# Moving the down projection of the last 512 rows into the blocked products at the end, with another layout for the query weight scan

## The chip, the cores and the metric

The kernel runs on one core of a Trainium2 chip. Its time is device microseconds from one execution; what is compared is the median of several. Five engines work beside each other, each through its own queue in order: TensorE (PE, matrix products; PEld is its weight load), VectorE (DVE), ScalarE (ACT), GpSimd (POOL) and SyncE (SP, which only issues DMAs here). They meet through semaphores.

## The reference, cut to what matters

```
x  = A_x                                  # 2048 x 640, bf16
xn = layernorm(x)
# A: attention, 32 heads of 192, over the last 512 keys of the cache
q  = xn @ wq                              # 640 -> 32 * 192
s  = softmax(q k^T / sqrt(192)) v  @ wo   # 6144 -> 640
# B: gated block, F = 1536
h  = sigmoid(xn @ w_gate) * (xn @ w_up)   # 2048 x 1536
g  = silu(h @ w_down)                     # 1536 -> 640, the down projection
out = x + s * g
```

All inputs and the output are bf16.

## The kernel before

The kernel has three parts, and PE goes through them one after the other.

**Gates (lines 275 to 581).** The 2048 rows are taken in four lots `s` of 512 rows. For each lot the 12 blocks `f` of 128 gate columns are computed: ten products of 128 x 512 into a pair of PSUM banks (line 487), then a sigmoid on ACT (L492) and a multiplication on DVE (L493), which writes the tile `hT_sb`. A ring of four bank pairs (`bank2`) lets PE run ahead of ACT and DVE. The tile `hT_sb` has two buffers. For the first three lots the h rows are stored to the tensors `h_d` in memory (L550, and L530 for the third lot), and their down projection is done at the end of the kernel. For the fourth lot the down projection follows at once (L556 to L581): 96 products with `hT_sb` as weights and `wd_sb` as moving operand, a sigmoid into `sg`, a multiplication into `gB_sb`, and a DMA to `gB_d`.

Beside the gates other work is hung on steps `(s, f)` by small tables written out by hand, so the order of each engine's queue is the order of the code:

- `ln_at`: layer norm of the next lot; `ln_rest` (L438) turns the rows by a DMA transpose into `xnT`, which is in the tile `x_odd` for odd lots.
- `scan_load`, `scan_fold`, `scan_act`: the largest magnitude of the query weights is needed for a scale. Sixteen blocks of `wq` are loaded (L201) and reduced, on DVE (`scan_fold`) or as a sum of magnitudes on ACT (`scan_abs`, L300). `set_scale` turns the result across partitions with a small DMA transpose, `set_scale2` makes the scale `w_up`.
- `load_raw`, `scale_w`, `sum_w`: each of five chunks of a group's query weights is loaded (L230), scaled to fp16 (L244 and two copies, L249) and combined into sums (four operations on DVE, L262 to L266, and a copy on ACT). Queries are computed by a Winograd form of Strassen's blocked product, which needs these sums and those of x.
- `swap` and `sum_x`: the sums of x for two lots together, six operations of 64 x 2560 each on DVE.
- `load_k`, `scale_k`, `turn_k`, `load_v`: keys and values of the first group.

In the fourth lot, chunk 4 of the weights, two scalings for the next group (`scale_raw(1, ...)`) and three sums of x stand between the parts of the down projection (L569 to L577).

**Attention (lines 614 to 969).** Sixteen runs, one for each of 8 groups and 2 halves of the rows. Each computes scores (L700), exponentials (L704), the product with the values (L714), and the queries of the next run (L606, with evacuations at L625, L627 and L644). The queries of the first run are computed ahead of it, by `query_slots(0, True, ...)` at L772: there the copies are on ACT, and PE has the banks 2 and 3, 4 and 5, 0, 1 and 6. The tiles of this part (`qT`, `qp`, `E`, `o_st`, `oT`) lie in memory that the tiles of the gates had.

**Dense end (from line 971).** A list `steps` of blocked products, seven quarter products in place of eight: `O` steps for the output projection (7 x 12 products of 128 x 320 each), `D` steps for the down projection of two row tiles (7 x 6 products). `load_quads` loads the operands two steps ahead, `scale_quad` and `sum_quad` scale and combine them, `result` evacuates; for `D` steps it makes a gate and stores it to `gB_d`. Other work is hung on positions of the steps with `at`: `load_op`, `scale_op`, `sum_op` for the second half of the output weights, `pair_load` and `prep` for the gate and x rows of each tile.

```
steps = [(k[0], int(k[1:])) for k in "O0 O1 D0 D1 O2 D2 D3 O3 D4 D5 O4 O5 O6 O7".split()]
...
        if kind == "D":
            return (m, TQ + m) if m < TQ else (2 * m, 2 * m + 1)
```

Of the kernel before, what the change touches and what calls it, by code (L numbers as in the profile page):

```python
# [8 lines left out]
AF = mybir.ActivationFunctionType  # L9
ALU = mybir.AluOpType  # L10
# [7 lines left out]
def kernel(  # L18
# [75 lines left out]
    NH, NM3 = NF // 2, 3  # L94
    h_d = [dram.tile([P, NF, P], BF16, name=f"h_d{t}") for t in range(NM3 * TQ)]
# [51 lines left out]
    wq_n = A_wq.rearrange("(c p) n -> p c n", p=P)  # L147
# [42 lines left out]
    NPC, NSB = 16, 7  # L190
    NSC = NG * GC // NPC
    assert NSC <= GC // 2

    def scan_load(i, eng):
        n = i % NSB
        if n < 3:
            t = (XA, XB, XC)[n][1]
            scan_t[i] = (t if n == 2 else t.bitcast(BF16))[:, :, 0:NSC]
        else:
            scan_t[i] = w_even[n - 3].bitcast(BF16)[:, :, 0:NSC]  # L200
        eng.dma_start(scan_t[i], wq_n[:, :, i * NSC:(i + 1) * NSC])  # L201
# [73 lines left out]
    with ExitStack() as bctx:  # L275
# [4 lines left out]
        gpool = bctx.enter_context(tc.tile_pool(name="gpool", bufs=4))  # L280
# [10 lines left out]
        x_odd = xt_pool.tile([P, NCD, 512], BF16, name="x_odd")  # L291
        xnT = [x_even[0], x_odd, x_even[1], x_odd]

        wmax = bone.tile([P, NCD, NSC], BF16, name="wmax")
# [46 lines left out]
        wd_sb = wB.tile([P, NF, D], BF16, name="wd_sb")  # L341
# [101 lines left out]
        def swap(pi):  # L443
            x_sw = xt_pool.tile([P, 2, NCD, 512], BF16, name="x_sw")
            nc.sync.dma_start(XC[pi][LO], x_odd[HI])
            nc.sync.dma_start(XC[pi][HI], x_odd[HI])
            nc.sync.dma_start(x_sw[HI, 0], x_even[pi][LO])
            nc.sync.dma_start(x_sw[HI, 1], x_odd[LO])
            return x_sw

        def sum_x(pi, k, x_sw):
            ev, od, tt = x_even[pi], x_odd, nc.vector.tensor_tensor
            xa, xb = XA[pi], XB[pi]
            if k == 0:
                tt(xa[LO], od[LO], XC[pi][LO], ALU.add)
            elif k == 1:
                tt(xa[HI], od[HI], x_sw[HI, 1], ALU.add)
            elif k == 2:
                tt(xa[LO], xa[LO], ev[LO], ALU.subtract)
            elif k == 3:  # L460
                tt(xb[HI], xa[HI], x_sw[HI, 0], ALU.subtract)
            elif k == 4:
                tt(xb[LO], ev[LO], od[LO], ALU.subtract)
            elif k == 5:
                tt(xb[HI], ev[HI], xb[HI], ALU.subtract)

        sums = {(1, 4): (0, 4), (1, 10): (0, 0), (1, 11): (0, 1), (2, 7): (0, 2), (2, 9): (0, 3), (2, 10): (0, 5),
                (3, 2): (1, 0), (3, 4): (1, 1), (3, 7): (1, 2)}
        folds = {(1, 7): 9, (1, 8): 10, (1, 9): 11}
        scan_act = {(0, 7): 0, (0, 8): 1, (0, 9): 2, (0, 10): 3, (1, 1): 4, (1, 2): 5, (1, 3): 6, (1, 6): 7, (1, 7): 8,  # L470
                    (2, 0): 12, (2, 1): 13, (2, 5): 14, (2, 7): 15}
        scan_loads = {(0, 8): (4, 5, 6), (0, 9): (7,), (0, 10): (8,), (0, 11): (9,), (1, 1): (10, 11), (1, 7): (12, 13), (1, 9): (14, 15)}
        abs_at = [(0, 3), (0, 4), (2, 9), (2, 10)]
        ln_at = {0: (2, (1, 1, 2), 5), 1: (0, (1, 1, 1, 1), 4), 2: (0, (1, 1, 1, 1), 4)}
        for s in range(NST):
# [4 lines left out]
            for f in range(NF):  # L480
# [31 lines left out]
                if (s, f) in folds:  # L512
                    scan_fold(wmax, folds[s, f], folds[s, f] == 9)
# [8 lines left out]
                if s == 2 and f == 8:  # L522
                    nc.vector.tensor_reduce(
                        scans[:, 0:1], wmax[:].rearrange("p c n -> p (c n)"), axis=mybir.AxisListType.X, op=ALU.max)
                    set_scale(scans[:])
                elif s == 2 and f == 11:
                    set_scale2()
                elif s == 3 and f == 1:
                    for q in range(TQ):
                        nc.sync.dma_start(h_d[2 * TQ + q][:], h_last[:, q, :, :])  # L530
                    nc.sync.dma_start(wd_sb[:], B_w_down.rearrange("(f p) d -> p f d", p=P))
                elif s == 3 and f == 5:
                    for hp in range(G):
                        load_v(0, hp, nc.sync)
                if s == 3:
                    for c in {0: (0,), 2: (1,), 5: (2,), 8: (3,)}.get(f, ()):
                        scale_w(0, c)
                    for c in {1: (0,), 3: (1,), 6: (2,), 9: (3,)}.get(f, ()):
                        sum_w(0, c)
                        load_raw((c + 3) // NCD, (c + 3) % NCD, nc.gpsimd)  # L540
                    if f in (0, 7):
                        scale_k((0, f // 7))
                    elif f in (3, 9):
                        turn_k((0, f // 9))
                    if f == 0:
                        load_k((0, 1), nc.gpsimd)
            if s < NM3:
                h_last = hT_sb
                for q in range(TQ) if s < 2 else ():
                    nc.sync.dma_start(h_d[s * TQ + q][:], hT_sb[:, q, :, :])  # L550
                if s == 1:
                    for c in range(3):
                        load_raw(0, c, nc.sync)
                    load_k((0, 0), nc.sync)
                continue
            for q in range(TQ):  # L556
                oB_ps = flat(bank2())
                for f in range(NF):
                    for d0, dsz in d_chunks:
                        nc.tensor.matmul(  # L560
                            oB_ps[:, d0:d0 + dsz], lhsT=hT_sb[:, q, f, :],
                            rhs=wd_sb[:, f, d0:d0 + dsz],
                            start=(f == 0), stop=(f == NF - 1),
                        )
                gB_sb = gpool.tile([P, D], BF16, name="gB_sb")
                sg = bone.tile([P, D], F32, name="sg")
                nc.scalar.activation(sg[:], oB_ps[:, 0:D], AF.Sigmoid)
                nc.vector.tensor_tensor(gB_sb[:], oB_ps[:, 0:D], sg[:], ALU.mult)
                if q == 0:  # L569
                    scale_w(0, NCD - 1)  # L570
                elif q < 3:
                    scale_raw(1, q - 1)
                if q == 1:
                    sum_w(0, NCD - 1)
                    load_raw(1, 2, nc.gpsimd)
                if q < 3:
                    sum_x(pi, 3 + q, sw)  # L577
                else:
                    load_k((1, 0), nc.gpsimd)
                t = s * TQ + q  # L580
                nc.gpsimd.dma_start(gB_d[t * P:(t + 1) * P, :], gB_sb[:])  # L581
# [191 lines left out]
    for n, k in enumerate((0, 1, 7, 2, 3, 8, 4, 5, 9, 6, 10)):  # L773
        slots[k]()
        if n == 0:
            nc.scalar.activation(mx, w_up, AF.Exp, scale=0.0)
        if n < 2:
            second_w(n)
# [18 lines left out]
    steps = [(k[0], int(k[1:])) for k in "O0 O1 D0 D1 O2 D2 D3 O3 D4 D5 O4 O5 O6 O7".split()]  # L797
# [8 lines left out]
    def tiles_of(j):  # L806
        kind, m = steps[j]
        if kind == "D":
            return (m, TQ + m) if m < TQ else (2 * m, 2 * m + 1)
        pi, q = divmod(m % 8, TQ)  # L810
        return [(2 * pi + i) * TQ + q for i in range(2)]
# [43 lines left out]
    def phase_s(r, pi, g, k, q_list, pv_list):  # L855
# [5 lines left out]
        if pi == 0 and g + 1 < NG:  # L861
            if k == 2 and g > 0:
                load_k((g + 1, 0))
            elif k == 12:
                scale_k((g + 1, 0))
                load_k((g + 1, 1))
# [225 lines left out]
    for key, j in (("O2", 0), ("O2", 3), ("O3", 1), ("O4", 2)):  # L1092
        at(key, 0, load_op, 1, j)
    for key, p, n in (("O3", 6, 0), ("O3", 8, 3), ("O4", 1, 4), ("O5", 1, 5)):
        at(key, p, scale_op, 1, n)
    for n, (key, p) in enumerate((("O4", 7), ("O5", 3), ("O6", 3), ("O7", 3))):
        at(key, p, sum_op, 1, n)
    prep_at = [("O2", 8), ("O3", 1), ("O3", 3)]
    prep_at += [(f"O{m}", 8) for m in (4, 4, 5, 5, 6, 6, 7, 8, 9, 10, 11, 12, 13)]
    for n, (key, p) in enumerate(prep_at):  # L1100
        if n < 6:
            at(("O2", "O2", "D2", "O3", "D4", "D4")[n], 0, pair_load, 0, n, first)
    for n, (key, p) in enumerate(prep_at):
        at(key, p, prep, n)
        if 6 <= n + 3 < len(prep_at):
            at(key, p, pair_load, 0, n + 3, first)
# [108 lines left out]
```

## Time and profile before

| what | value |
|---|---|
| median of 3 runs | 873.76 us (873.42 to 873.94) |
| profiled execution, its own time | 874.75 us |
| its span, first to last instruction | 873.0 us |
| PE busy | 865.2 us, 99% |
| DVE busy | 674.6 us, 77% |
| ACT busy | 625.4 us, 72% |
| POOL busy | 212.1 us, 24% |
| moved by DMA | 174.69 MB, mean 200 GB/s |
| gates, products of L487 | 15.69 to 112.60 us |
| down projection of the last lot, L560 | 112.60 to 125.82 us |
| dense end, L1022 | from 652.27 us |

The span is cut from one execution under the profiler; its own time is 1.75 us longer than its span. A busy time is a sum over instructions of an engine. "Idle before, with releaser" says how long an engine stood still ahead of an instruction and what ended that.

### The profile page before, as it was taken

To read this page: it belongs to the slowest core of one execution; us is meant where nothing else is said; L and a number is where in the kernel's file an instruction comes from. 1 tells how busy PE (TensorE), PEld (TensorE's weight loads), DVE (VectorE), ACT (ScalarE), POOL (GpSimd) and SP (SyncE) were. 2 spreads that over 40 slices of the span, in tenths; PEclk is the share of its full clock that TensorE was granted. 3 is DMA by queue.
4 is the path that set the end of the run, shared out by engine and by line. 5 is a ranking of instruction groups with operands and counts; after the bars stand their busy time and mean duration, and the time that the engine had idled before them with its cause. 6 is when DMAs were issued, how large, how long until landed. Compare 5 with 4: busy or idle time off the path is not lost.

```text
span 873.0 us, 18973 instructions
## 1 busy us (share of the span) xinstructions
PE 865.2 (99%) x7558; PEld 567.2 (65%) x7569; DVE 674.6 (77%) x1137; ACT 625.4 (72%) x772; POOL 212.1 (24%) x299
## 2 busy tenths in 40 slices
PE   8999999999999999999999999999999999999998
PEld 5444445756756756756756756756777777777776
DVE  6587777777777677677677777787978587989997
ACT  5868676488788788788788787774655667666662
POOL 0000239406407407407407406300000111000000
PEclk9999999999999999999999999999999999999999
DMA  9998982599789799699789779597788888566841
GB/s 269 269 279 223 267 178 55 85 243 177 179 219 189 143 253 190 141 249 171 161 226 175 158 182 202 126 292 207 200 209 222 256 275 269 154 225 206 279 164 38
DMA packets 264712, 174.69 MB, mean 200 GB/s; under 512 B 162256, under 2 KB 249680, under 8 KB 264624
## 3 DMA queue, kind: packets, MB, share of 16 engines
q1 hardware_dynamic: 258192, 153.23, 68.6%
q0 software_dynamic: 6432, 20.26, 11.5%
q8 instruction: 59, 0.97, 0.5%
q14 instruction: 29, 0.24, 0.1%
HBM read 102.11 MB, written 35.13 MB: 157 GB/s over the span
## 4 chain that ended last, share of the span: by engine, by line
PE 95%; ACT 1%; DMA 1%; DVE 1%; SPq 1%; issue 0%; ACTq 0%; DVEq 0%
PE ps_all L1022 24%; PE ps_all L714 20%; PE ps_all L606 19%; PE ps_all L700 18%; PE ps_all L487 11%; PE ps_all L560 1%; DMA kraw<-in_A_k_cache_dram 1%; ACT E L704 1%; PE ps_all L395 1%; DMA x_sb<-in_A_x_dram 1%; ACT arm L759 0%; SPq L158 0%; DVE arm L1006 0%; DVE arm L1077 0%; SPq L330 0%
## 5 line engine op out<-in xcount | busy, mean ns | idle before, releaser
L704 ACT ACTIVATE E<-ps_all 128x1024 bf16<-128x1024 f32 x256 | 251.2, 1022 | 114.4 <-PE ps_all L700 113.7
L700 PE MATMUL ps_all<-qT,kT 64*128 64x512 bf16 x1536 | 198.1, 376 | 0.0
L714 PEld LDWEIGHTS <-E 128*128 128x128 bf16 x2048 | 169.7, 98 | 8.9 <-issue 8.9
L714 PE MATMUL ps_all<-v_sb,E 128*128 128x193 bf16 x2048 | 174.1, 247 | 0.7 <-DVE qT L644 0.7
L644 DVE TENSOR_TENSOR qT<-ps_all,qp 128x512 bf16<-128x512 f32 x174 | 115.5, 687 | 48.4 <-PE ps_all L606 36.8
L1022 PEld LDWEIGHTS <-mid 128*128 128x128 f16 x1176 | 115.0, 98 | 44.6
L700 PEld LDWEIGHTS <-kT 64*128 64x128 bf16 x1536 | 84.9, 94 | 79.5 <-issue 4.4
L627 DVE COPY qp<-ps_all 128x512 f32<-128x512 f32 x150 | 100.5, 686 | 45.7 <-PE ps_all L606 45.7
L721 DVE TENSOR_TENSOR o_st<-ps_all,rden 128x768 bf16<-128x768 f32 x128 | 122.5, 957 | 4.4
L606 PE MATMUL ps_all<-mid 64*128 64x512 f16 (+1 forms) x840 | 106.2, 376 | 0.4 <-DVE qT L644 0.4
L606 PE MATMUL ps_all<-mid,arm 64*128 64x512 f16 (+1 forms) x840 | 105.6, 376 | 0.0
L606 PEld LDWEIGHTS <-mid 64*128 64x128 f16 x840 | 49.0, 94 | 43.8 <-issue 1.8
L606 PEld LDWEIGHTS <-arm 64*128 64x128 f16 x840 | 47.1, 94 | 44.6 <-issue 0.2
L1022 PE MATMUL ps_all<-arm,mid 128*128 128x320 f16 x462 | 67.5, 299 | 0.0
L835 ACT ACTIVATE mid<-mid,w_sc 128x1536 f16<-128x1536 bf16 (+1 forms) x41 | 60.2, 1493 | 0.0
L244 ACT ACTIVATE mid<-mid,w_sc 128x1536 f16<-128x1536 bf16 x37 | 58.2, 1573 | 1.9 <-DVE w_sc L222 1.3
L1022 PE MATMUL ps_all<-op,mid 128*128 128x320 f16 x378 | 55.1, 299 | 0.0
L493 DVE TENSOR_TENSOR hT_sb<-ps_all,sig_sb 128x512 bf16<-128x512 f32 x48 | 32.7, 684 | 26.1 <-ACT sig_sb L492 17.7
L230 POOL DMA_DIRECT2D mid<-in_A_wq_dram x74 | 43.9, 598 | 21.9 <-DVE mid L266 19.2
L1022 PE MATMUL ps_all<-mid 128*128 128x320 f16 x336 | 48.3, 299 | 0.0
L262 POOL TENSOR_TENSOR arm<-mid 128x384 f16<-128x384 f16 x20 | 18.1, 904 | 115.6 <-ACT mid L244 114.5
L720 DVE RECIPROCAL rden<-ps_all 128x4 f32<-128x4 f32 x128 | 23.3, 182 | 28.1 <-PE ps_all L714 26.7
(185 smaller groups left out, 1057.2 us busy)
## 6 DMA issues: line engine op xcount, KB each, us to landing
oT_d<-oT SPq DMA_DIRECT2D x64, 384.0 KB, 5.6
mid<-oT_d SPq DMA_DIRECT2D x46, 384.0 KB, 5.0
mid<-in_A_wq_dram POOLq DMA_DIRECT2D x74, 192.0 KB, 6.4
mid<-in_A_wq_dram SPq DMA_DIRECT2D x16, 480.0 KB, 7.7
arm<-in_A_wo_dram SPq DMA_DIRECT2D x16, 480.0 KB, 5.7
v_sb<-in_A_v_cache_dram SPq DMA_DIRECT2D x32, 192.0 KB, 6.4
kraw<-in_A_k_cache_dram SPq DMA_DIRECT2D x28, 192.0 KB, 4.0
h_d<-hT_sb SPq DMA_DIRECT2D x12, 384.0 KB, 7.2
```

Source lines behind the costliest of these rows:

```text
L230: eng.dma_start(raw[r], wq_r[:, c, :, g * GC:(g + 1) * GC])
L244: nc.scalar.activation(raw.bitcast(F16), raw, AF.Copy, scale=w_up)
L487: nc.tensor.matmul(gu[:, i, :], lhsT=w[:, c, f * P:(f + 1) * P], rhs=xnT[s][:, c, :], start=(c == 0), stop=(c == NCD - 1),)
L606: nc.tensor.matmul(ps_all[:, b, :], lhsT=w(r, c), rhs=x[r, c, :], start=(first and k == 0), stop=(k == len(cs) - 1), skip_group_check=True,)
L627: nc.vector.tensor_copy(dst, part(b))
L644: nc.vector.tensor_tensor(q_out(i, u, pp), part(b), t, ALU.add)
L700: nc.tensor.matmul(ps[:, b, :], lhsT=kT[h, c * PC + j, :], rhs=qT_t[r][i, j][h, pp, :], start=(j == 0), stop=(j == PC - 1),)
L704: nc.scalar.activation(E_t[r, i, pp][:, c, :, :], ps, AF.Exp, scale=scale_qk)
L714: nc.tensor.matmul(o_ps[:, q // 2, q % 2, 0:DH + 1], lhsT=E[:, c, h, q * P:(q + 1) * P], rhs=vt[:, c, 0:DH + 1], start=(c == 0), stop=(c = ...
L721: nc.vector.tensor_tensor(o_st[:, :, h * DH:(h + 1) * DH].rearrange("p (b i) d -> p b i d", b=2), o_ps[:, :, :, 0:DH], rden[:].to_broadcas ...
L835: eng.activation(t, t.bitcast(BF16), AF.Copy, scale=up)
L1022: nc.tensor.matmul(ps_all[:, b, d0:d1], lhsT=a[:, c, :], rhs=w[:, c, d0:d1], start=(start and c == 0), stop=(c == nk - 1), skip_group_chec ...
```

## The change

It has three parts that belong together. The last lot's h rows are stored like the others (`store_h`), and its down projection becomes two more steps, D6 and D7, between O4 and O5; the direct form, `wd_sb` and the tiles `gB_sb` and `sg` are gone. The steps' row tiles are paired anew (`tiles_of`), and the loads, scalings, sums and preparations on the positions of O2 to O7 are spread differently. The scan of the query weights reads the weights as contiguous rows of 1920 elements for each partition in place of five pieces of 384, into other buffers (eleven in place of seven); it ends in step (2, 2), and the scale is made in (2, 3) to (2, 6). So the first two chunks of query weights are prepared in the third lot, and the three others, the two scalings for the next group and all six sums of x for the second half of the rows in the fourth. There are two tiles for odd lots of turned rows, `x_odds`, in place of one. Stores of h rows, loads of keys and values and one scaling of keys have other places.

```diff
-    wq_n = A_wq.rearrange("(c p) n -> p c n", p=P)
+    wq_n = A_wq.rearrange("(p c) n -> p (c n)", p=P)
...
-        x_odd = xt_pool.tile([P, NCD, 512], BF16, name="x_odd")
-        xnT = [x_even[0], x_odd, x_even[1], x_odd]
+        x_odds = [xt_pool.tile([P, NCD, 512], BF16, name=f"x_odd{pi}") for pi in range(2)]
+        xnT = [x_even[0], x_odds[0], x_even[1], x_odds[1]]
...
-                (3, 2): (1, 0), (3, 4): (1, 1), (3, 7): (1, 2)}
+                (3, 2): (1, 0), (3, 3): (1, 1), (3, 5): (1, 2), (3, 8): (1, 3), (3, 9): (1, 4), (3, 10): (1, 5)}
...
-        abs_at = [(0, 3), (0, 4), (2, 9), (2, 10)]
+        abs_at = [(0, 3), (0, 4), (2, 4), (3, 4)]
+        scale_at = {(2, 7): 0, (2, 9): 1, (3, 0): 2, (3, 3): 3, (3, 6): 4}
+        sum_at = {(2, 8): 0, (2, 10): 1, (3, 1): 2, (3, 4): 3, (3, 7): 4}
+        raw_at = {(3, 8): 0, (3, 10): 1}
...
+        def store_h(s, hT_sb):
+            for q in range(TQ):
+                nc.sync.dma_start(h_d[s * TQ + q][:], hT_sb[:, q, :, :])
...
+                if (s, f) in ((1, 1), (2, 4), (3, 1)):
+                    store_h(s - 1, h_last)
...
-            for q in range(TQ):
-                oB_ps = flat(bank2())
-                for f in range(NF):
-                    for d0, dsz in d_chunks:
-                        nc.tensor.matmul(
-                            oB_ps[:, d0:d0 + dsz], lhsT=hT_sb[:, q, f, :],
-                            rhs=wd_sb[:, f, d0:d0 + dsz],
-                            start=(f == 0), stop=(f == NF - 1),
-                        )
-                gB_sb = gpool.tile([P, D], BF16, name="gB_sb")
-                sg = bone.tile([P, D], F32, name="sg")
-                nc.scalar.activation(sg[:], oB_ps[:, 0:D], AF.Sigmoid)
-                nc.vector.tensor_tensor(gB_sb[:], oB_ps[:, 0:D], sg[:], ALU.mult)
...
+            h_last = hT_sb
+        store_h(NST - 1, h_last)
...
-        if n == 0:
+        if n == 1:
             nc.scalar.activation(mx, w_up, AF.Exp, scale=0.0)
...
-    steps = [(k[0], int(k[1:])) for k in "O0 O1 D0 D1 O2 D2 D3 O3 D4 D5 O4 O5 O6 O7".split()]
+    steps = [(k[0], int(k[1:])) for k in "O0 O1 D0 D1 O2 D2 D3 O3 D4 D5 O4 D6 D7 O5 O6 O7".split()]
...
-            return (m, TQ + m) if m < TQ else (2 * m, 2 * m + 1)
+            return (m, TQ + m) if m < TQ else (TQ + m, 2 * TQ + m)
...
-            if k == 2 and g > 0:
+            if k == 2:
                 load_k((g + 1, 0))
-            elif k == 12:
+            elif k == (14 if g == 1 else 12):
                 scale_k((g + 1, 0))
...
-    for n, (key, p) in enumerate((("O4", 7), ("O5", 3), ("O6", 3), ("O7", 3))):
+    for n, (key, p) in enumerate((("O5", 1), ("O6", 1), ("O6", 6), ("O7", 3))):
         at(key, p, sum_op, 1, n)
```

## The prediction

> **What bounds the kernel now.** I read the page first: the share of each engine, and the chain that ended last.
>
> ```profile
> PE 865.2 (99%) x7558; PEld 567.2 (65%) x7569; DVE 674.6 (77%) x1137; ACT 625.4 (72%) x772; POOL 212.1 (24%) x299
> PE 95%; ACT 1%; DMA 1%; DVE 1%; SPq 1%; issue 0%; ACTq 0%; DVEq 0%
> ```
>
> TensorE (PE) is the bound, so a microsecond is won by taking PE work away and lost by making PE wait. Next, what PE waited for (first column after the colon: us in total).
>
> ```profile
> PE ps_all L385 <- DVE warm L379: 1.3, 1, 1.3
> PE ps_all L714 <- DVE qT L644: 0.7, 1, 0.7
> PE ps_all L408 <- DVE xn L372: 0.4, 1, 0.4
> PE ps_all L606 <- DVE qT L644: 0.4, 1, 0.4
> PE ps_all L395 <- ACT mid L410: 0.3, 1, 0.3
> ```
>
> Behind the start only 0.7 and 0.4 us are left to win, so any new wait shows in full. The chain in order of time (start, us, what) gives the rates.
>
> ```profile
> 102.24 10.52 PE ps_all L487 x48
> 113.09 6.82 PE ps_all L560 x49
> 119.96 5.94 PE ps_all L560 x43
> 131.02 7.24 PE ps_all L606 x64
> 652.27 211.91 PE ps_all L1022 x1560
> ```
>
> A dense-end product takes 211.91/1560 = 0.1358 us, a half-array query product 7.24/64 = 0.113 us. Last the timeline around the stage that goes, with the landing times of h_d stores (lines L530 and L550).
>
> ```profile
> 107.95 0.69 DVE L493 TENSOR_TENSOR hT_sb<-ps_all,sig_sb 128x512 bf16<-128x512 f32 x1 [0.42 <-ACT sig_sb L492]
> 112.60 13.28 PE L560 MATMUL ps_all<-wd_sb,hT_sb 128*128 128x512 bf16 x94
> 117.73 1.49 DVE L461 TENSOR_TENSOR mid<-mid,x_sw 64x2560 f16<-64x2560 f16 x1
> 125.82 4.84 PE L606 MATMUL ps_all<-mid 64*128 64x512 bf16 x41
> 127.64 0.60 ACT L625 ACTIVATE qp<-ps_all 128x512 f32<-128x512 f32 x1 [1.02 <-DVE gB_sb L568]
> ```
> ```profile
> DMA to landing us min/median/max: 6.0/7.2/7.7
> DMA to landing us min/median/max: 6.7/7.1/7.9
> ```
>
> Between 112.60 and 125.82 the down products (L560) kept PE busy while VectorE (DVE) and ScalarE (ACT) finished gates, query weights and sums of x. That stage is work, but also cover.
>
> **PE work.** Removed: 96 products, 112.60 to 125.82, 13.22 us. Added: steps D6 and D7, 2 x 7 x 6 = 84 products at 0.1358, 11.41 us. Net -1.81 us, all on the path. Their loads, scalings, sums and gates come twice more; the existing pair D4, D5 (720.7 to 732.1) uses 9.61 us of DVE and 7.18 of ACT beside 11.40 of PE and shows no PE wait, so I take 0. But DVE is busy 11.30, 11.26 and 11.05 of 11.4 us in O5, O6, O7 of before: if a moved sum_op (2.15 us, L753) lands too late the cover is gone. Bounds 0 to +2.2.
>
> **The stall at 226.8.** PE waited 0.7 us because DVE stood 1.17 us in scale_k of group 2 for the key load, with the query additions queued behind. Two score steps later (k = 14; two times 12 products of L700 at 1.29 us) the load has landed: -0.7, bounds -0.7 to 0.
>
> **Weight scan and other early edits.** The same sixteen blocks of 480 KB, as 128 runs of 3840 bytes instead of 640 of 768: fewer packets, no PE wait hangs on them (the one wait for a scan load was ACT's, 2.0 us). The scale comes five f steps sooner, so weight chunks 0 and 1 move from the fourth 512 rows to the third, and chunk 4 from L560 to the fourth. In the third, ACT was busy 20.04 and DVE 20.72 of 25.9 us (60.8 to 86.7); two scale_w (2.6 each) and two copies (0.5) against one scan and one abs_up (2.0 each) fit ACT, two sum_w (1.5 each) fit DVE. Both fall further behind PE, but PE has spare bank pairs for two to three f steps of 2.16. I take 0; if the fourth 512 rows start with more arrears, up to +0.7. On SyncE (SP) the turns of x for the last rows now stand behind mx_row's turn and four h stores: the last of before was issued at 80.1 and landed at 84.4, 2.3 us ahead of its first use; were that cover gone, the wait below would swallow most of it. The two x_odd buffers only remove a reuse wait that PE does not have. Two key loads change their queue or place; group 1's has ten score steps, 13 us, against 4.0 to land. All 0.
>
> **Where the cover goes.** The last h tile is now stored too, four DMAs on SP right after its last multiplication. The built program shows what follows: in front of the first copy of a query product on ACT, and of the first addition on DVE, stand waits for the stores of both h buffers, those four included, since the query tiles take their memory. In the program before, the same copy waits for the stores of rows 1024 to 1535, landed by 100.6, and for the last gB_sb multiplication. Everything behind these two instructions on ACT and DVE waits too, and with them PE, when its banks are full.
>
> When can the stores go? DVE's queue from the multiplication of f = 7 on: it started at 107.95 in before. In the new order follow sum_w of chunk 4 (106.01 to 107.52 for the same four operations, 1.52), scale_k 0.73, and then a 1.49 sum of x ahead of each of the last three multiplications (they stood beside L560): 0.65 + 1.52 + 0.73 + 0.65 + 1.49 + 0.65 + 1.49 + 0.65 + 1.49 + 0.69 = 10.0, so the last one ends at 118.0 (114.31 + 1.29 = 115.6 before). SP issues stores 0.48 apart, the fourth at 118.0 + 3 x 0.48 = 119.4. Landing: the twelve h_d rows have 6.0 to 7.9, in a busier stretch; the shortest median of a 384 KB move in the page is 4.4. I take 6.0, the shortest of the h_d rows, since less else is loaded by then: 125.4. The copy (0.60) frees the first bank at 126.0; the addition after it (0.69) frees the second, where before has a wait of 0.35 at the same place: +0.3.
>
> PE ends the gates at 112.6, can do three query slots into free banks, 30 x 0.113 = 3.4, to 116.0, and then must have the first banks back. It loses 126.0 - 116.0 + 0.3 = 10.3 us (partly already at 114 to 118, when the last gates free their banks late). Bounds: 8.7 with a landing in 4.4; 12.9 with 7.9 and the +0.7.
>
> [...]
>
> **A slow restart.** After its idle time at the start PE issues 512-column products 427 ns apart (nine up to 5.16), the same shape later 216. Nowhere else in this trace does PE idle for microseconds. A wait of over 7 us in one piece is nearest to that row: half rate for about 4 us is at most 2.0 lost; some of it falls where PE would wait for evacuations anyway, so I take +1.5, bounds 0 to 2.0.
>
> [...]
>
> **The sum.** -1.81 - 0.7 + 10.3 + 1.5 = +9.3 us. The profiled execution has 874.75 us, 873.0 of span and 1.75 around it, and lies 1.0 above the median of 873.76; its span would become 882.3, its time 884.05, and the median 883.1.
>
> **Rivals.**
> 1. Faster: the stores are hidden, only the first terms stay. It needs PE to get its banks by 118.5, so a landing before 117.9; but with PE's last gate product at 112.6, then a sigmoid (0.60) and a multiplication (0.69), stores cannot start before 113.9, and 4.4 after that is 118.3 for the first. For it speaks PE's 99% share and the saved 1.81; against it the waits in the built program. -2.5, 871.3 us.
> 2. The store wait, but no slow restart: 881.6. For: the profile's granted clock is 1.00 even at the start.
> 3. More comes late: DVE is the bound in O5 to O7 (+2.2), or ACT and DVE are 0.7 later and the landing takes 7.9 (+2.6): 885.3 to 887.9. For: DVE at 99% there; against: moved preps and scalings were spread.
> 4. The wait is mostly covered: DVE and ACT keep up (last multiplication done at 113.9, fourth store issued at 115.3) and the stores land in 4.0 like a 192 KB key load, at 119.3. The bank is free at 119.9, 3.9 are lost: +1.4, 875.2, within 0.2% of before. Against it the 10.0 us of DVE worked out above.
> The change surely does what it says: 84 products stand for 96 in the built program.
>
> **Chances.** Forecast 0.55, rival 2 0.25, rival 3 0.14, rival 4 0.03, rival 1 0.03. A difference of 0.2%, 1.75 us, is about what a measurement of this kernel can tell from no change. Faster 0.03, same 0.03, slower 0.94. The range: low, 8.7 lost and no slow restart, 873.76 - 2.5 + 8.7 = 880.0, and half a microsecond for a DVE that runs less behind: 879.5; high, the upper part of rival 3, 888.0.
>
> **What would show it.** Right: PE's products in the dense end 84 more at the same 0.136 us, ending without new waits; a wait of PE of 7 us or more between 114 and 128 us, ended by ACT's copy to qp, itself released by h_d stores that were issued near 118; query products at half rate behind it; no wait near 225 (226.8 - 13.2 + 11.8). Wrong: no such wait, h_d landing ahead of the first copy, or a loss in O4 to O7 larger than that at 120.

## The result, and the profile after

| kernel | median | runs |
|---|---|---|
| before | 873.85 us | 873.42 to 873.94 |
| after | 886.73 us | 885.92 to 887.36 |

The changed kernel is slower: ratio 1.0145, 95% interval 1.0132 to 1.0157. The forecast was 883.1, with a range of 879.5 to 888.0. Its profiled execution took 887.34 us, 885.6 of it span, so the span grew by 12.6 us.

The page of the changed kernel first: busy time of the engines, the lines of PE and of its granted clock in 40 slices of 22 us, and the chain that ended last.

```profile
PE 868.2 (98%) x7548; PEld 568.9 (64%) x7557; DVE 679.7 (77%) x1153; ACT 629.3 (71%) x784; POOL 211.8 (24%) x293
...
PE   9999959999999999999999999999999999999998
...
PEclk9999979999999999999999999999999999999999
...
PE 84%; issue 1%; DVE 1%; ACT 0%; ACTq 0%; DVEq 0%
```

What went wrong sits in one slice, the sixth (111 to 133 us): PE is half idle there, and its granted clock falls as well. PE's busy total rose by 3 us although 12 products are gone, in part because 24 query products ran at half rate (granted clock 0.50 from 122.68 to 132.92 us), which is about 2.5 us. The waits of PE between 104 and 131 us (us in total, times, longest) answer to the list shown of before; outside of them only short ones of the start and one of 0.2 us are left:

```profile
PE ps_all L584 <- ACT qp L603: 4.5, 1, 4.5
PE ps_all L584 <- DVE hT_sb L499: 4.3, 3, 2.8
PE ps_all L493 <- DVE hT_sb L499: 0.9, 1, 0.9
PE ps_all L493 <- ACT sig_sb L498: 0.6, 1, 0.6
PE ps_all L584 <- DVE qT L622: 0.2, 1, 0.2
```

(The lines have moved: gates L487 are now L493, their sigmoid L498 and multiplication L499, the query products L584, their copies L603 and additions L622, the stores L479.) The first is of the kind that was forecast: a query product waits for ScalarE's copy. But the forecast's sign was one wait of 7 us or more, on stores issued near 118 us; this one is 4.5 us, on stores issued at 122.8 us. The second was not in the sum as a loss of its own: PE waits 4.3 us for VectorE's last gate multiplications. The timeline shows both, one behind the other:

```profile
118.26 1.62 DVE L460 TENSOR_TENSOR mid<-mid,x_odd 64x2560 f16<-64x2560 bf16 x1
...
120.52 1.49 DVE L462 TENSOR_TENSOR mid<-mid 64x2560 f16<-64x2560 bf16 x1
...
122.04 0.69 DVE L499 TENSOR_TENSOR hT_sb<-ps_all,sig_sb 128x512 bf16<-128x512 f32 x1
122.76 2.32 SPq L479 DMA_DIRECT2D h_d<-hT_sb  x4
122.78 2.29 PE L584 MATMUL ps_all<-mid 64*128 64x512 bf16 x9 [2.85 <-DVE hT_sb L499]
...
128.90 1.08 ACT L603 ACTIVATE qp<-ps_all 128x512 f32<-128x512 f32 x2 [9.39 <-issue]
129.55 0.58 PE L584 MATMUL ps_all<-mid 64*128 64x512 f16 x1 [4.47 <-ACT qp L603]
```

The last multiplication started at 122.04, with sums of x (L460, L462) between it and its predecessors. Its stores went out at 122.76, and the copy on ACT started at 128.90. The landing times in the trace of the four stores are 125.09, 126.09, 127.08 and 128.67, so ACT stood until the fourth had landed. The timeline puts only "issue" beside the 9.39 us; the view of the tile `h_d` names that copy as the one that waited 9.4 us for it.

From marks in both traces the loss adds up. The last gate product started 2.5 us later than before (114.93 against 112.39); 1.5 of that are the two waits of L493 above. From there to the first score it took 24.6 us; before, without the 13.2 of the direct products, 12.3. So 2.54 + (24.64 - 12.31) = 14.9 us were lost between the gates and the first score. Of those, 8.9 are waits at the query products (0.52 + 0.90 + 2.85 + 4.47 + 0.20), about 2.5 are products at half rate, and the last 1 us was not taken apart. Against that stand 13.22 saved, 11.41 spent in the dense end, 0.85 for the stall at 226.8 that is gone (first score to dense start is 513.3 us, 514.2 before), and 0.4 more at the very end: 14.9 - 13.2 + 11.4 - 0.85 + 0.4 = 12.6.

The dense end did as forecast. Its piece of the chain answers to that of before:

```profile
653.07 223.32 PE ps_all L1000 x1644
```

223.32/1644 is 0.1358 us for a product, the same as before, and no PE wait stands in O4 to O7.

### The profile page after: what moved, and what is told of

Read it like the earlier page. It is cut to its first block, busy times and chain, and to the rows that moved or that the text cites. A ratio compares the mean times of both kernels' runs of the same rounds, so it can differ in the third digit from the quotient of the medians.

```text
span 885.6 us, 19009 instructions
## 1 busy us (share of the span) xinstructions
PE 868.2 (98%) x7548; PEld 568.9 (64%) x7557; DVE 679.7 (77%) x1153; ACT 629.3 (71%) x784; POOL 211.8 (24%) x293
## 4 chain that ended last, share of the span: by engine, by line
PE 84%; issue 1%; DVE 1%; ACT 0%; ACTq 0%; DVEq 0%
PE ps_all L1000 25%; PE ps_all L584 20%; PE ps_all L692 20%; PE ps_all L678 19%; DVE arm L984 0%; DVE arm L1055 0%; DVE arm L1053 0%; DVE qT L622 0%; ACT qp L603 0%; ACTq L603 0%; DVEq L622 0%; DVEq L1053 0%
## 5 line engine op out<-in xcount | busy, mean ns | idle before, releaser
L622 DVE TENSOR_TENSOR qT<-ps_all,qp 128x512 bf16<-128x512 f32 x174 | 115.5, 687 | 54.5 <-PE ps_all L584 36.8
L1000 PEld LDWEIGHTS <-mid 128*128 128x128 f16 x1236 | 120.3, 98 | 46.0
L584 PE MATMUL ps_all<-mid 64*128 64x512 f16 (+1 forms) x840 | 109.8, 383 | 8.9 <-ACT qp L603 4.5
L584 PE MATMUL ps_all<-mid,arm 64*128 64x512 f16 (+1 forms) x840 | 105.6, 376 | 0.0
L584 PEld LDWEIGHTS <-mid 64*128 64x128 f16 x840 | 49.9, 95 | 55.3 <-issue 15.2
L584 PEld LDWEIGHTS <-arm 64*128 64x128 f16 x840 | 47.1, 94 | 44.6 <-issue 0.2
L1000 PE MATMUL ps_all<-arm,mid 128*128 128x320 f16 x480 | 70.4, 299 | 0.0
L1000 PE MATMUL ps_all<-op,mid 128*128 128x320 f16 (+1 forms) x408 | 58.1, 295 | 0.0
L499 DVE TENSOR_TENSOR hT_sb<-ps_all,sig_sb 128x512 bf16<-128x512 f32 x48 | 32.8, 684 | 26.3 <-ACT sig_sb L498 17.0
L227 POOL DMA_DIRECT2D mid<-in_A_wq_dram x70 | 41.7, 598 | 13.4 <-DVE mid L263 13.4
```

What stands on the lines that cost most here:

```text
L227: eng.dma_start(raw[r], wq_r[:, c, :, g * GC:(g + 1) * GC])
L499: nc.vector.tensor_tensor(hT_sb[:, :, f, :], *(v.rearrange("p (q n) -> p q n", q=TQ) for v in (gu[:, 1, :], sig_sb[:])), ALU.mult,)
L584: nc.tensor.matmul(ps_all[:, b, :], lhsT=w(r, c), rhs=x[r, c, :], start=(first and k == 0), stop=(k == len(cs) - 1), skip_group_check=True,)
L622: nc.vector.tensor_tensor(q_out(i, u, pp), part(b), t, ALU.add)
L1000: nc.tensor.matmul(ps_all[:, b, d0:d1], lhsT=a[:, c, :], rhs=w[:, c, d0:d1], start=(start and c == 0), stop=(c == nk - 1), skip_group_chec ...
```

## The experiments

Two questions were open: how much is the store wait and how much the lateness of VectorE and ScalarE; and where does the lateness come from. Each kernel does all of the work. Times stand against the kernel before on the same chip: 873.65 us (experiments 1 to 3), 874.12 (4 to 6, on another chip) and 873.88 (7).

**1. The store wait taken away.** The query copies wait for the last four h stores, although in the built program the bytes of the last lot's buffer are reused by the exponentials only (the tiles `qT` and `qp` overlap the other buffer). What they wait for is the pool's room: `hpool` reaches into the room where `qT_pool` and `qp_pool` lie later. Moving one line puts it elsewhere.

```diff
-        hpool = bctx.enter_context(tc.tile_pool(name="hpool", bufs=2))
         xpool = bctx.enter_context(tc.tile_pool(name="xpool", bufs=4))
         xin_pool = bctx.enter_context(tc.tile_pool(name="xin_pool", bufs=1))
+        hpool = bctx.enter_context(tc.tile_pool(name="hpool", bufs=2))
```

> The changed kernel with one line moved: the pool of the gate outputs (hpool) is allocated behind the pools of the x rows, so that its room is later taken by the exponentials' pool and no longer by the pools of the query copies and the turned queries. The first copy of a query product and the first query sum then need no store to have landed. Theory 1 (the 14.9 us lost around the last gates and the first query products are two things: TensorE held 4.7 us by copies and sums that wait for the four stores, and some 8 us by VectorE and ScalarE being late with the gates): the waits of 4.47 and 0.20 us at 125 to 130 us go, and half of the 2 us of slow products with them, so 880 to 882 us; a wait of 2 to 4 us for the last multiplications stays. Theory 2 (the stores alone, as the record's sum has it, 10.3 of 11.8 us): 873 to 876 us. Theory 3 (late engines alone, the stores land in their shadow): 885.5 to 887 us.

Measured: 881.78 us, ratio 1.0094 (1.0079 to 1.0109), 5.0 under the changed kernel. Its waits of PE at the last gates and behind them:

```profile
PE ps_all L584 <- DVE hT_sb L499: 4.3, 3, 2.8
PE ps_all L493 <- DVE hT_sb L499: 1.0, 1, 1.0
PE ps_all L493 <- ACT sig_sb L498: 0.6, 1, 0.6
...
```

The waits on `qp` and `qT` are gone and the others are the same to 0.1 us. The pool's place made the store wait, and it is not the whole loss: theory 1 gave 880 to 882 us, and theories 2 and 3 fall.

**2. The direct products put back.** The rest of the change is kept up to the attention; the places of loads, sums and preparations in the dense end go back with the two steps.

```diff
-        store_h(NST - 1, h_last)
+        for q in range(TQ):
+            oB_ps = flat(bank2())
+            ...
-"O0 O1 D0 D1 O2 D2 D3 O3 D4 D5 O4 D6 D7 O5 O6 O7"
+"O0 O1 D0 D1 O2 D2 D3 O3 D4 D5 O4 O5 O6 O7"
```

> The other way round: the down projection of the last 512 rows stays where it was (96 products straight after the gates, no store of the last lot, six dense steps D), with all else of the change: scan in contiguous rows, two buffers for odd turned rows, weight scalings and sums in lots 2 and 3. Down weights lie in the room of the scan's spare buffers, and the gated rows have three buffers instead of four. Theory 1: the late VectorE and ScalarE cost TensorE 4 to 7 us at the last gates and at the first direct products, which need the last multiplications; stores cost nothing: 877 to 881 us. Theory 2 (stores alone): the 0.85 us stall goes, 873 us. Theory 3 (late engines alone, all of the 14.9 us): 884 to 888 us.

Measured: 879.62 us, ratio 1.0066 (1.0051 to 1.0081).

```profile
PE ps_all L567 <- DMA more<-in_B_w_down_dram: 2.1, 1, 2.1
PE ps_all L567 <- DVE hT_sb L501: 1.8, 1, 1.8
...
```

L567 is the direct product here. So the new order of scan, weights and sums costs some 6 us with no store in play. The wait of 2.1 for the down weights is a blemish of this kernel, but little of the result hangs on it: the products then stood a second time, until 122.25, for the last multiplication, which ended at 122.19, nearly as late as in the changed kernel (122.73).

**3. The last lots made lighter, at first the wrong way.** The weight sums of group 0 go to GpSimd, sums of x move to earlier steps, one scaling goes into the query products; then the same with `hpool` moved.

```diff
-                    sum_w(0, c)
+                    sum_w(0, c, nc.gpsimd.tensor_tensor, nc.gpsimd.tensor_copy)
...
+(3, 0): (1, 4), (3, 2): (1, 0), (3, 4): (1, 1), (3, 5): (1, 2), (3, 6): (1, 3), (3, 8): (1, 5)}
...
-        raw_at = {(3, 8): 0, (3, 10): 1}
+        raw_at = {(3, 8): 0}
```

> The changed kernel with its pools as they were, but with less work on VectorE and ScalarE in the last two lots: the five weight sums of group 0 and the copy among them go to GpSimd, the sum of x that needs no swap goes to the start of lot 3, the others a step or two earlier, and the second scaling of raw weights of group 1 into the first query products. The stores still hold the query copies. Theory 1 (late engines and stores): the last multiplication ends at 115 to 117 us instead of 122.7, the stores land 5.9 us after that as before, TensorE goes on at about 122 to 124 instead of 129.6 us: 879 to 882 us, and one wait of 5 to 7 us for the first query copy is left. Theory 2 (the stores alone, with the lateness no loss of its own): the wait for the first query copy grows by as much as the wait for the multiplication shrinks only if TensorE is at the same point; TensorE goes on at 125 us at the earliest, 883 us. Theory 3 (late engines alone): 873 to 875 us.

> Both edits together: the pool moved and the work of the last two lots spread. Theory 1: neither wait is left; 1.8 us less work for TensorE and the 0.85 us stall at 226.8 gone against the kernel before, with 0.5 to 2.5 us of short waits left: 871.5 to 874.5 us. Theory 2 gives the same as for the pool alone, 873 to 876; theory 3 the same as for the spread work alone, 873 to 875. Were the losses neither of the two, but more work at the end, it would be over 878.

Measured: 894.11 us, ratio 1.0235 (1.0218 to 1.0252), and with the pool moved 883.39, ratio 1.0116 (1.0083 to 1.0149). The first is outside what any theory gave; the second falls under "over 878", which was to mean more work at the end. The timeline of the first shows another cause, the order of SyncE's queue, in two places:

```profile
95.39 1.59 SPq L227 DMA_DIRECT2D mid<-in_A_wq_dram  x2
...
97.08 0.56 SPq L442 DMA_DIRECT2D mid<-x_odd  x1
...
104.78 1.72 DVE L452 TENSOR_TENSOR mid<-x_odd,mid 64x2560 f16<-64x2560 bf16 x1 [8.99 <-DMA mid<-x_odd]
...
107.15 2.29 PE L493 MATMUL ps_all<-x_odd,wu_sb 128*128 128x512 bf16 x5 [3.71 <-DVE hT_sb L499]
...
120.89 6.12 SPq L172 DMA_TRANSPOSE kT<-k_sb  x1
127.11 2.65 SPq L479 DMA_DIRECT2D h_d<-hT_sb  x4
...
135.77 0.58 PE L587 MATMUL ps_all<-mid 64*128 64x512 f16 x1 [12.49 <-ACT qp L606]
```

First, SyncE's queue holds a load of raw weights (L227), which waits until a weight sum has freed its buffer. On GpSimd that sum ended at 96.3 instead of 93.4 us. Behind the load stood the swap of x (L442), behind the swap a sum of x on VectorE, for 8.99 us, and behind that the gate multiplications, for which PE stood 3.71 us. Second, and dearer: the last multiplication had ended at 121.70, but a transpose of keys (L172) held SyncE until 127.01, so the stores went out only at 127.11, and PE stood 12.49 us for the first query copy. In the changed kernel that transpose held SyncE for 1.88 us; why it took longer here is open. In the second kernel the same transpose held the stores back to 126.74, and the first exponential waited 4.47 us for them: with the pool moved, the wait had passed to the exponentials. So these two kernels say little about the theories.

**4. That load on another queue.** The kernel of experiment 1, and one more line:

```diff
-                    load_raw((c + 3) // NCD, (c + 3) % NCD, nc.sync if s == 2 else nc.gpsimd)
+                    load_raw((c + 3) // NCD, (c + 3) % NCD, nc.gpsimd)
```

> The kernel with hpool moved (881.78 us), and the two loads of raw weights of lot 2 issued by GpSimd's queue instead of SyncE's, where the second waits for a weight sum (93.1 us in the changed kernel) and holds up the swap of the odd turned rows behind it (issued 94.5 to 96.8, landed 99.4 to 104.6, and VectorE waited 1.67 us for it ahead of a sum of x, with four multiplications behind that). If SyncE's order is part of VectorE's lateness: the swap is issued by 91, the wait of 1.67 us goes, the last multiplication ends 1 to 3 us earlier than 122.1, and the time is 878 to 880.5 us. If the lateness is only the amount of work on VectorE and ScalarE: 881.3 to 882.3 us, the last multiplication at 122.

Measured: 879.05 us, ratio 1.0056 (1.0041 to 1.0071), 2.7 under experiment 1. First the swap in SyncE's queue in the changed kernel, then here:

```profile
93.12 1.31 SPq L227 DMA_DIRECT2D mid<-in_A_wq_dram  x2
94.52 0.55 SPq L442 DMA_DIRECT2D mid<-x_odd  x1
```
```profile
86.18 0.54 SPq L442 DMA_DIRECT2D mid<-x_odd  x1
```

The swap went out 8 us earlier, as expected (by 91 us), and the last multiplication ended at 119.74 instead of 122.14. SyncE's order is part of the lateness; 119.74 is still late.

**5. Lighter lots without weight sums on GpSimd, with the pool moved and with the pool back.** Both kernels keep the load on GpSimd's queue from experiment 4. Only the one copy inside each weight sum goes to GpSimd; the sum of x that needs no swap comes first, the last one and one scaling go into the query products.

```diff
-                    sum_w(0, c)
+                    sum_w(0, c, copy=nc.gpsimd.tensor_copy)
...
-                (3, 2): (1, 0), (3, 3): (1, 1), (3, 5): (1, 2), (3, 8): (1, 3), (3, 9): (1, 4), (3, 10): (1, 5)}
+                (3, 0): (1, 4), (3, 2): (1, 0), (3, 4): (1, 1), (3, 5): (1, 2), (3, 8): (1, 3)}
...
-        raw_at = {(3, 8): 0, (3, 10): 1}
+        raw_at = {(3, 8): 0}
...
-        if n < 2:
-            second_w(n)
+        if n == 6:
+            scale_raw(1, 1)
+        if n == 3:
+            sum_x(1, 5, sw)
+        if n in (0, 7):
+            second_w(n // 7)
```

> The kernel with hpool moved and the raw loads of lot 2 on GpSimd's queue, and lighter last lots: the one copy inside each weight sum of group 0 goes to GpSimd (ScalarE waited 1.4 us for VectorE ahead of it, five times), the sum of x that needs no swap to the start of lot 3, the last one and the second raw scaling of group 1 into the first query products; the weight sums stay on VectorE. All work is done, with the same result. If the loss is the store wait and the late engines: the last multiplication ends at 115 to 118 us, no wait of over 1 us and no slow spell is left at the first query products, the first score is at 126 to 128 us: 872 to 875 us, possibly below the kernel before (873.65). If the last 14 us were bound by the amount of work on VectorE (about 23 us in the 26 us of lot 3), it stays over 878 us.

> The kernel e6 with hpool back in its place: only the store wait is left. The stores go out when the last multiplication ends (115 to 118), land 5.9 us later as measured, and the first copy takes 0.6 us; TensorE stands from about 115.5 to 122 to 124 us: 6.5 to 9 us over e6 with the slow spell that follows, 879 to 883 us. If the stores mattered only because the last multiplication came late, it stays within 2 us of e6.

Measured: with the pool moved 874.11 us (871.41 to 878.98), ratio 1.0004 (0.9986 to 1.0021); with the pool back 883.94, ratio 1.0103 (1.0081 to 1.0126). The first median lies where it was expected, but its profiled execution (877.54 us) still had a wait of PE of 1.54 us and a slow spell (granted clock 0.998 over the whole of it), its last multiplication ended at 119.09 us and its first score came at 129.71, later than expected. In the second the store wait stands nearly alone (the waits of PE for the last gates sum to 1.0 us):

```profile
117.27 2.94 SPq L479 DMA_DIRECT2D h_d<-hT_sb  x4
...
124.87 1.08 ACT L603 ACTIVATE qp<-ps_all 128x512 f32<-128x512 f32 x2 [8.35 <-DMA h_d<-hT_sb]
125.52 0.58 PE L584 MATMUL ps_all<-mid 64*128 64x512 f16 x1 [6.98 <-ACT qp L603]
```

This is the forecast's mechanism at nearly its numbers: stores at 117.3, the copy 7.6 us after the first of them, PE standing 7.0 us. It costs 883.94 - 874.11 = 9.8 us, a little more than the 6.5 to 9 expected. So these four medians make a square:

| | last lots as changed | last lots lighter |
|---|---|---|
| stores waited for | 886.73 | 883.94 |
| pool moved | 881.78 | 874.11 |

Each loss hides part of the other. The stores cost 5.0 us beside late engines and 9.8 alone; the lateness (with the raw load's queue in it) 2.8 us beside the store wait and 7.7 alone. The medians come from three series; taken against the kernel before of each, the four differences are 4.8, 9.8, 3.1 and 8.1. The lower right median stands for runs from 871.41 to 878.98, so the figures in which it enters hold to about 1.5 us.

**6. The keys' scaling two steps later, alone.** The kernel before, with the edit for group 1 of the change only (`k == (14 if g == 1 else 12)`).

> The kernel before with one edit of the change alone: the scaling of the next keys moved from step 12 to 14 for the second group. The 0.85 us wait of TensorE at 226.8 us goes: 872.8 us (0.1% less). If another wait takes its place: 873.65 us.

Measured: 873.77 us against 874.12, ratio 0.9998 (0.9989 to 1.0007). The trace no longer has the wait at 226.8 and its span is 872.0 (873.0 before), but the median expected, 872.8, was not reached, and the medians do not tell the gain from none.

**7. What is left.** The runs of experiment 5 with the pool moved spread over 7.6 us. In the profiled one ScalarE waited 5.61 us for a raw load of the next group, with the last sigmoids behind it. Two kernels: values loaded later, and then that scaling moved into the query products too.

```diff
-                    elif f == 6:
-                        for hp in range(G):
-                            load_v(0, hp, nc.sync)
...
         store_h(NST - 1, h_last)
+        for hp in range(G):
+            load_v(0, hp, nc.sync)
```
```diff
-        raw_at = {(3, 8): 0}
+        raw_at = {}
...
-        if n == 6:
-            scale_raw(1, 1)
+        if n in (2, 6):
+            scale_raw(1, n // 6)
...
-        if n in (0, 7):
+        if n in (3, 7):
```

> The kernel e6 (874.11 us, runs from 871.4 to 879.0) with the four loads of values for group 0 behind the stores of the last lot in SyncE's queue instead of at step 6 of lot 3, so that they no longer share the DMA engines with the raw weights and keys of that time: in the profiled run of e6 (877.5 us) ScalarE waited 5.6 us for a raw weight load at 114.9 and VectorE 1.9 us for keys, and the last multiplications stood behind both. If that sharing is what is left of the loss: both waits go, the last multiplication ends at 115 to 117 instead of 119.1 us, and the time is 871.5 to 873.5 us, below the kernel before. If those loads are late for another reason (GpSimd issues the raw load only after the third weight sum): 874 us as e6.

> The kernel e9 with the first raw scaling of group 1 in the query products too, so that no step of lot 3 waits for a raw load of group 1, whichever the reason for its late landing. Theory (what lies ahead of the last multiplications on ScalarE and VectorE sets the loss): no wait of over 1 us at the first query products other than short ones for ScalarE's copies, which now share it with two scalings of 1.6 us: 871.5 to 873.5 us and closer runs than e6's. If ScalarE becomes the bound of the query products: 1 to 2 us more than e9.

Measured: 874.23 us, ratio 1.0012 (1.0003 to 1.0021), and 872.54 us (872.2 to 876.53), ratio 0.9993 (0.9983 to 1.0003). The first line below is from the first of them: the raw load was as late as ever, though the values no longer shared its time.

```profile
113.10 1.58 ACT L241 ACTIVATE mid<-mid,w_sc 128x1536 f16<-128x1536 bf16 x1 [5.25 <-DMA mid<-in_A_wq_dram]
```

So sharing with the values was not the reason. With the scaling moved away as well, PE goes from 16 us on through the gates and the first queries with one wait over 0.15 us:

```profile
112.70 6.73 PE L583 MATMUL ps_all<-mid 64*128 64x512 bf16 x60
119.67 5.57 PE L583 MATMUL ps_all<-mid 64*128 64x512 f16 x45 [0.24 <-ACT qp L602]
124.90 1.46 PE L677 MATMUL ps_all<-qT,kT 64*128 64x512 bf16 x11
```

The first score is at 124.9 us: 14.7 earlier than in the changed kernel (139.57), and 13.0 earlier than before (137.92). That is all of the loss, with the move of the down projection and the layout of the scan still in. The median is 1.3 us under the kernel before; the interval does not quite exclude no gain. As all of the work now fits without loss, the loss was one of order, engine and place; which of the moved pieces was worth how much this does not say.

## Why the prediction was right, and where its sum was off

Direction was right, and the store wait exists as described; the median came out 3.6 us higher than forecast. That it stayed inside the range is in part luck: the store wait, taken away by itself, gave back 5.0 us where the sum had 11.8 for it and the restart, and the lateness of VectorE and ScalarE, which the sum had at 0, filled the gap. The wait of 7 us or more that was to show the mechanism came only in experiment 5, where the lateness was nearly gone.

- **PE work, -1.81.** Right: 84 products more at 0.1358 us in the dense end, 11.41, and 96 gone.
- **Dense end 0, bounds 0 to +2.2.** Right as to waits: the moved `sum_op`, `prep` and loads made none. The tail behind the last product is 0.4 us longer, which was not in the sum. With this rival 3 loses the first of its two halves.
- **The stall at 226.8, -0.7.** Right: the wait of that size is gone in the profile.
- **The store wait, +10.3, and the slow restart, +1.5.** The mechanism is shown by moving the pool, and nearly alone it costs 9.8 us in all, against 11.8. In the changed kernel it came to 5.0, as half of it was hidden behind a wait that the sum did not have. The landing of the fourth store was put at 7.4 us behind the end of the last multiplication; it was 5.9 in the changed kernel, and in experiment 5 the copy that waited for it started 7.6 us behind that end.
- **Rate after the wait.** It did come: from 122.68 to 132.92 us, after the wait of 2.85 us and through that of 4.47, the granted clock is 0.50 and pairs of query products stand 427 ns apart instead of 216, for about 2.5 us of loss where the sum had 1.5. In the line, busy times of PE, its weight load, DVE, ACT and POOL stand first, then the clock, DMA share and GB/s.

```profile
122.68:132.92 10.24, 5.46 (x24) 1.84 (x25) 2.03 (x4) 3.72 (x7) 9.53 (x15) 0.50 0.80 230
```

The argument for rival 2, a granted clock of 1.00 even at the start, was no evidence: the clock's record in the changed kernel's trace begins at 6.62 us, behind the slow products of the start, and nothing was known there.

- **Arrears of VectorE and ScalarE, 0, at most +0.7.** This is the term that was mis-sized. The queue's sum put the end of the last multiplication at 118.0; it was 122.73, 4.7 us later. The sum began at 107.95, with the multiplication of f = 7 where before had it; in the changed kernel that multiplication was already 4.5 us late:

```profile
112.47 0.69 DVE L499 TENSOR_TENSOR hT_sb<-ps_all,sig_sb 128x512 bf16<-128x512 f32 x1 [1.13 <-ACT sig_sb L498]
```

From there to the end it took 10.26 us, against 10.0 in the sum, so the queue behind that point was worked out well, and its starting point was wrong. The step had compared busy times with the 25.9 us of the third lot and concluded that the added work fits. The third lot shows the flaw, before and after (DVE and ACT are the third and fourth busy times):

```profile
60.80:86.70 25.90, 25.80 (x119) 11.72 (x120) 20.72 (x38) 20.04 (x27) 0.00 (x0) 1.00 0.89 245
60.80:86.70 25.90, 25.60 (x118) 11.69 (x120) 18.86 (x40) 17.59 (x23) 0.00 (x0) 1.00 0.81 215
```

More was planned there, and less was done: there was room by busy time, but the engines stood in waits between their queues. ScalarE waited 2.39 us for a scan load (2.0 in before) and 1.94 for the scale (1.3), and VectorE 2.54 and 2.71 us for sigmoids of ScalarE; in the fourth lot VectorE waited 1.67 for the swap. Inside the weight sums ScalarE waited 1.4 to 1.6 us for VectorE five times (four in before). What was left undone came on top in the fourth lot. The step looked at SyncE's queue for the turns of x, but not for the raw load that waits for a weight sum ahead of the swap (2.7 us in experiment 4). The last kernel of experiment 7 keeps the scan as the change has it and loses nothing at the end, so the bunching of scan blocks at the start of the third lot does not by itself cost time there. How the 4.5 us split between these waits and the moved work, and how much each of the moved sums, copies and scalings cost by itself, was not measured.

The total fits: gates and first queries 14.9 against 11.8, plus 0.4 of tail and minus 0.15 of stall, is the 3.3 us between 884.05 and 887.34 for the profiled execution. Rival 3 had the size (885.3 to 887.9) and part of the cause, late engines; its late landing and its bound in O5 to O7 did not come.

## What to carry to other kernels

A stage that is moved away was also a cover: list what ran beside it, and for each piece which instruction now waits for it, on which queue, and what stands behind that; a share of busy time below 100% does not say that in-order engines which wait for each other keep up (here VectorE was busy 18.86 and ScalarE 17.59 of 25.9 us in the third lot, and the multiplication of f = 7 in the fourth came 4.5 us late). When a buffer gets a new late reader (here a store), look at whose memory it is given to next: the wait can go by the pool's room and not by the bytes, and one line that moves the pool can take it away (4.47 us of PE's waiting, experiment 1), or hand it to whoever gets the room instead (4.47 us at the first exponential in experiment 3). Two losses at one place hide each other, so removing either shows less than it costs alone (the stores 5.0 us against 9.8): try both, and both together.

## What the runs showed of the hardware

**When TensorE falls to half rate.** In its wait of 2.85 us the changed kernel's granted clock fell to 0.50, at 122.68 us, and stayed there until 132.92. In experiment 3, five products behind a wait of 3.71 us took 2.29 us instead of 1.24 (first kernel), and ten query products behind a wait of 3.62 us at the first scores took 2.37 us, against 1.42 ahead of it (second kernel). In experiment 1, with a wait of 2.84 us, the clock was 0.81 in the mean from 115 to 133 us. Over the whole profiled execution it was 0.988 in experiment 3's first kernel, with waits of 3.71 and 12.49 us, 0.995 in experiment 4, where the longest wait was 2.3 us, and 0.998 in experiment 5's first kernel, with 1.54; but 1.000 in experiment 2, with waits of 2.06 and 1.80 us, and in experiment 7's first kernel, with 1.6. In the second kernel of experiment 3 a wait of 3.10 us was followed by full rate (five products in 1.24 us are 216 ns apart):

```profile
106.17 1.24 PE L493 MATMUL ps_all<-x_odd,wu_sb 128*128 128x512 bf16 x5 [3.10 <-DVE hT_sb L499]
```

So the length of the last wait alone does not decide, and what does was not shown. In the changed kernel's trace the clock falls at 122.68 us, rises at 132.92 and falls again at 883.85, behind the last product: 10.24 and 750.93 us apart, which is 3 and 220 times 3.413. In the 3.41 us ahead of the first fall PE had worked 0.67 us. No run was made to settle this.

**GpSimd and VectorE beside each other.** An operation of GpSimd that took 0.91 us in the other weight sums beside the gates took 2.04 beside a sum of x on VectorE, itself 1.98 us instead of 1.49 (experiment 3, first kernel):

```profile
86.26 1.98 DVE L458 TENSOR_TENSOR mid<-mid,x_sw 64x2560 f16<-64x2560 f16 x1
86.97 2.04 POOL L263 TENSOR_TENSOR mid<-mid 64x384 f16<-64x384 f16 x1
```

Longer steps like these are a second reason why handing weight sums to GpSimd did not help: in the sum that ended at 96.3 us, two of five steps took 2.25 and 1.98 us beside sums of x that took 1.49 and 1.48, where the same steps of the sum before it took 0.91 and 0.50. Why the operations lengthen each other was not shown.
